# Windowed attention and a rational feed-forward layer on one core: the first 50 transfers of the load queue each wait for an earlier one to land

## The chip, the core and the metric

The kernel runs on one core of a Trainium2 chip. A core has a matrix engine (PE, with its weight loads PEld), two elementwise engines that read PE's accumulators (DVE and ACT), a third that works on on-chip memory only (POOL), and a sequencer (SP) from which this kernel issues all of its data transfers. The metric is the device time of one launch in microseconds, as a median over runs.

## The reference

Eight batches of eight heads of attention, 576 positions of 64 values, each query seeing at most 32 keys (the last 32 positions in the first four heads, every fourth of the last 128 in the other four). The result, 4608 tokens of 512 values, goes through a feed-forward layer with a rational activation.

```python
scores = scale * np.matmul(q, k.transpose(0, 1, 3, 2))
...
scores = np.where(masks[None, :, :, :], scores, -1000000000.0)
...
attn = attn / (np.sum(attn, axis=-1, keepdims=True) + 1e-09)
return np.matmul(attn, v).astype(np.float32)
...
h = x @ w_in
...
P = a[0] + a[1] * h + a[2] * h2 + a[3] * h3
Q = 1.0 + np.abs(b[0]) * np.abs(h) + np.abs(b[1]) * h2
g = P / (Q + 1e-06)
return (g @ w_out).astype(np.float32)
```

The weights w_in (512 x 2048) and w_out (2048 x 512) arrive in 64 bit.

## The kernel before

**Tiling.** Attention is cut into 48 units, six to a batch. A unit loads a tile `qk` (448 KB) and a tile `v`, PE makes the scores into the accumulator tile `pair` (`pair_A` and `pair_B` in the first batch), DVE and ACT make the softmax, PE turns the weights (`t`) and multiplies by `v`, and the result is split into a high and a low part, `xh` and `xl`. The feed-forward layer is cut into 144 tiles: 12 matmuls make `h` (512 tokens by 128 hidden values), ACT, DVE and POOL make the activation, split into `gh` and `gl`, and 12 matmuls add it into four accumulators `out`. All matmuls of that layer run as three products of split values.

**Weights.** 32 slices of the weights (`wi_raw` and `wo_raw`, 512 KB each) are loaded in 64 bit. ACT scales the upper words (`wi_f<-wi_raw`), ACT or POOL scales the lower words (`wi_raw<-wi_raw`), DVE joins them, and two more operations split the result into a high and a low part.

**Order.** Every operation is an `Op` of a planner, class `Plan`. The table `ORDER` lists, by number, in which order operations are placed and, by a letter, on which engine; what it doesn't list is placed by the planner's own rule at the end. `place` calls the function that writes the instructions, so the program of each engine is in that order. The planner's model of time decides two further things: which of several equal buffers a tile gets (`held`), and how many filler matmuls `keep_busy` puts on PE where the model sees PE idle for longer than 0.25 us in the first 150 us (`idle`). Fillers write `ident_b` or zeros into an accumulator and change no result.

**Transfers.** `load` (line 337) issues a transfer on SP, in program order. A transfer waits for what it reads or overwrites; besides, the completion semaphores are eight, used in turn, and a transfer waits before it takes a semaphore of which the transfer eight places ahead has not landed. So up to eight transfers lie in the queue. The planner's model has the same limit, `FLYING = 8`, and a model of how PE's program is fetched in pages of 256 instructions: a page is asked for at one place of the program, comes `FETCH` later, and PE waits for it at another (`PAGE`, `ASK`, `LAST`).

Of the kernel before, what the change touches and what calls it, by code (L numbers as in the profile page):

```python
# [26 lines left out]
BOTH = {"ACT": 375, "DVE": 465}  # L27


START_S, START_O = ["A", "att"] * 3, ["B", "B", "B", "A", "B", "A"]  # L30
KIND = [0, 0, 0, 0, 1, 0] + [2] * 6
LESS = [0, 0, 0, 0, 1, 1]
# [73 lines left out]
1642 507 548 549 1671 550 1672 1656p 543 1639 551 552 1659 1658 508p 1660 1673a 1674d 538 1682 594 1677 1686 553 544 554 558 526 527p 559 565 555 560  # L106
566 567 613 1691 568 569 1657 1692 1693d 561 1678 1687 556 1675 1694 570 1696 1680 1695p 1697 1698 1689 571 1699 572 576 1700 1709 562 1690 1676 1701
573 1702 1681 1710 577 578 595 1711p 1713p 1727 579 1712 545 1714 1715 1703a 1704p 563 1716 574 1683 1717 1707 1728 584 546p 1718 1705 1708 1730 1706
632 1684 1729p 564p 1719 1720 1721a 1745 1732 1731p 580 1733
""".split()  # L110


class Op:
# [4 lines left out]
    def __init__(self, engs, rank, fn, deps, dma, lock):  # L118
        self.engs, self.rank, self.fn, self.dma, self.lock = engs, rank, fn, dma, lock
        self.deps = [d for d in deps if d is not None]  # L120
        self.takes, self.follows = [], []
        self.words, self.parts = 0, 1
        self.spare = None
        self.slack, self.by, self.end, self.eng, self.tail = None, None, None, None, 0.0
# [8 lines left out]
class Plan:  # L133
# [5 lines left out]
    DUE_HOP, WINDOW = 150.0, 200.0  # L139
    PE_START = 1500.0  # L140
    DMA_START, DMA_NS, DMA_RATE, DMA_FIRST = 1000.0, 1100.0, 355.0, 1100.0
    FLYING, PAGE, ASK, LAST, FETCH = 8, 256, 150, 449, 7400.0
    PERIOD, PE_LATE = 4743.0, 105.0

    def __init__(self, idle):
        self.ops, self.tags, self.idle, self.now = [], {}, idle, {}

    def op(self, engs, rank, fn, *deps, dma=0, lock=False, words=0, tail=0.0, parts=1):
        o = Op(engs, rank, fn, deps, dma, lock)
# [49 lines left out]
    def run(self, order):  # L199

        free, pages, flying = {}, [], []
        state = {"pipe": 0.0, "ports": 0.0, "words": 0, "left": len(self.ops)}
        left, after = {}, {}
        for o in self.ops:
            before = o.deps + [f for f in o.follows if f]
            left[id(o)] = len(before)
            for d in before:
                after.setdefault(id(d), []).append(o)
        ready = {id(o): o for o in self.ops if not left[id(o)]}

        def options(o):
            queue = []
            if o.dma:
                parts = 0
                for f in reversed(flying):
                    if parts + f.parts + o.parts > self.FLYING:
                        queue = [f.end]
                        break
                    parts += f.parts
            for eng, ns in o.engs.items():  # L220
                shared = state["ports"] if Plan.shares(o, eng) else 0.0
                held = [t for _, t, _ in self.held(o, eng)]
                start = max([free.get(eng, 0.0), shared] + queue + held + [d.after(eng) for d in o.deps])
                if start < math.inf:
                    yield start, o, eng, ns

        def fetched(start, ns, words):

            n0, n1 = state["words"], state["words"] + words
            for n in range(n0, n1):  # L230
                at = start + ns * (n - n0) / words
                if n % self.PAGE == self.ASK:
                    pages.append(at + self.FETCH)
                if n % self.PAGE == self.LAST - self.PAGE and n >= self.LAST and pages[n // self.PAGE - 1] > at:
                    ns += pages[n // self.PAGE - 1] - at
            state["words"] = n1
            return ns

        def place(start, o, eng, ns):
            self.now = {tag: n for tag, _, n in self.held(o, eng)}  # L240
            for tag, users in o.takes:
                self.tags[tag][self.now[tag]] = users
            o.eng = eng
            if eng == "PE":
                if start > free.get(eng, 0.0) + 1.0:
                    ns += self.PE_LATE
                    since = free.get(eng, self.PE_START)
                    fetched(since, start - since, 2 * self.idle(o, since, start))
                ns = fetched(start, ns, o.words)
            free[eng] = start + ns  # L250
            if Plan.shares(o, eng):
                state["ports"] = start + ns
            o.end = start + ns
            if o.dma:
                flying.append(o)
                state["pipe"] = max(state["pipe"], o.end + self.DMA_START) + o.dma / self.DMA_RATE
                if len(flying) == 3:
                    state["pipe"] += self.DMA_FIRST
                o.end = state["pipe"] + self.DMA_NS
            del ready[id(o)]  # L260
            state["left"] -= 1
            o.fn(eng)
            for n in after.get(id(o), []):
                left[id(n)] -= 1
                if not left[id(n)]:
                    ready[id(n)] = n

        for item in order:
            n, eng = (int(item[:-1]), ENGINES[item[-1]]) if item[-1] in ENGINES else (int(item), None)
            o = self.ops[n]  # L270
            assert id(o) in ready, "the order breaks a dependency"
            place(*next(x for x in options(o) if eng in (None, x[2])))
        while ready:
            every = [x for o in ready.values() for x in options(o)]
            assert every, "the plan is stuck"
            first = min(x[0] for x in every)
            eng0 = min((x for x in every if x[0] == first), key=lambda x: x[1].rank)[2]
            place(*min((x for x in every if x[2] == eng0 and x[0] <= first + self.WINDOW), key=lambda x: (x[1].rank, x[0])))
        assert not state["left"], "the plan is stuck"
# [3 lines left out]
def tile_attention_moe(  # L283
# [10 lines left out]
    nc = tc.nc  # L294
# [8 lines left out]
    pin = tc.keep_in_program_order  # L303
# [30 lines left out]
    plan = Plan(idle)  # L334
    op = plan.op

    def load(dst, src):
        pin(nc.sync.dma_start(dst, src))

    def mm(o, lhs, rhs, start=True, stop=True, free=False):  # L340
        pin(nc.tensor.matmul(o, lhs, rhs, start=start, stop=stop, skip_group_check=free))  # L341
# [44 lines left out]
    class Unit:  # L386
# [6 lines left out]
        def load_qk(self, pool, tag):  # L393
            t = pool.tile([P, RQ + RKEY], F32, tag=plan.at(tag), name=f"qk{self.n}", bufs=1)
            load(t, qk[self.n])
            self.q = t[:, :RQ].rearrange("p (g i c) -> p g i c", g=4, i=3)
            self.k = t[:, RQ:].rearrange("p (g k) -> p g k", g=4)

        def load_v(self, pool, tag):
            if self.n:  # L400
                self.v = pool.tile([P, NBAND if self.start else NV], F32, tag=plan.at(tag), name=f"v{self.n}", bufs=1)
                load(self.v, vb[self.n - 1] if self.start else vp[self.n - NU])
                return
            t = pool.tile([P, NBAND + NMASK + 6], F32, tag=tag, name="v0", bufs=1)
            load(t, head)
            self.v = t[:, :NBAND]
            extra["mask"] = t[:, NBAND : NBAND + NMASK].bitcast(BF16).rearrange("p (m k) -> p m k", k=64)
            extra["coef"] = t[:, NBAND + NMASK :]
# [857 lines left out]
```

## Time and profile before

| | |
|---|---|
| median of 3 runs | 893.29 us (890.53 to 895.08) |
| the profiled execution | 891.1 us, of which the span of its instructions is 889.1 us |
| granted PE clock | 1.00 of full speed |
| busy: PE, PEld, DVE, ACT, POOL | 875.1, 710.0, 722.9, 661.4, 499.7 us |
| moved by transfers | 102.63 MB, mean 115 GB/s over the span |

Busy time is counted from the span's start. A share over the whole span hides that the first 75 us are of another kind than the rest; stages have to be read by windows.

### The profile page before, as it was taken

The numbers are of one execution on the slowest core, as the hardware profiler recorded it, in microseconds if no ns is written. First come the engines' busy times: TensorE is split into PE (matmuls) and PEld (weight loads), VectorE is DVE, ScalarE is ACT, GpSimd is POOL, SyncE is SP. The second block draws the span as 40 slices with busy tenths as digits, with TensorE's granted clock in tenths as the row PEclk, the third lists the DMA queues.
The fourth block names the chain that finished last, engine by engine and source line by source line (L and its number), as shares of the span: only waits on it lengthen the run. The fifth ranks groups of instructions, "written<-read, shape, count | busy, mean of one in ns | idle before, by whom it ended". The sixth has DMA issues, their size and how long they took to land.

```text
span 889.1 us, 20736 instructions
## 1 busy us (share of the span) xinstructions
PE 875.1 (98%) x7991; PEld 710.0 (80%) x7991; DVE 722.9 (81%) x1285; ACT 661.4 (74%) x1104; POOL 499.7 (56%) x462
## 2 busy tenths in 40 slices
PE   7999999999999999999999999999999999999998
PEld 4777888888787888888888888888888887888886
DVE  6999899998898988888897889887666677667656
ACT  4999987776468876777776776777777787777764
POOL 4577767767565655556555464545554445444442
PEclk9999999999999999999999999999999999999999
DMA  9986451338853444443453435221200020001001
GB/s 349 344 260 204 175 203 36 105 109 244 247 157 101 137 139 148 128 134 114 149 162 96 134 107 175 79 80 38 81 11 1 1 71 1 1 1 47 1 1 47
DMA packets 85186, 102.63 MB, mean 115 GB/s; under 512 B 37216, under 2 KB 62560, under 8 KB 85088
## 3 DMA queue, kind: packets, MB, share of 16 engines
q1 hardware_dynamic: 85088, 101.32, 35.4%
q8 instruction: 62, 1.02, 0.5%
q14 instruction: 36, 0.29, 0.1%
HBM read 74.42 MB, written 26.87 MB: 114 GB/s over the span
## 4 chain that ended last, share of the span: by engine, by line
PE 84%; DVE 7%; ACT 4%; DMA 2%; issue 1%; POOL 1%; SPq 0%; DVEq 0%; ACTq 0%; POOLq 0%
PE out L341 40%; PE h L341 39%; PE pair L341 5%; DVE a L350 1%; ACT r L344 1%; DVE h L350 1%; ACT p L344 1%; PE pair_A L341 1%; DMA pT<-turned 1%; DVE xl L347 1%; ACT xh L344 1%; DVE t L347 0%; DMA results<-y 0%; DVE sm L489 0%; DVE wo_f L350 0%
## 5 line engine op out<-in xcount | busy, mean ns | idle before, releaser
L341 PE MATMUL h<-xh,wi 128*128 128x512 f32 x1136 | 376.7, 393 | 1.5 <-DVE a L350 1.3
L341 PE MATMUL out<-gh,wo 128*128 128x512 f32 x1136 | 351.9, 391 | 0.0
L353 POOL TENSOR_TENSOR a<-r,a 128x512 f32<-128x512 f32 x133 | 172.6, 1298 | 253.3 <-ACT r L344 230.1
L341 PEld LDWEIGHTS h<-xh,wi 128*128 128x128 f32 x1136 | 213.2, 188 | 50.4 <-DVE a L350 3.8
L341 PEld LDWEIGHTS out<-gh,wo 128*128 128x128 f32 x1136 | 211.9, 188 | 44.7
L350 DVE SCALAR_TENSOR_TENSOR a<-a,h 128x512 f32<-128x512 f32 x280 | 191.6, 684 | 61.9 <-POOL gl L353 37.8
L341 PE MATMUL h<-xl,wi 128*128 128x512 f32 x568 | 221.3, 390 | 0.0
L341 PE MATMUL out<-gl,wo 128*128 128x512 f32 x568 | 221.1, 389 | 0.0
L353 POOL TENSOR_TENSOR gl<-a,gh 128x512 fp32r<-128x512 f32 x134 | 177.3, 1323 | 41.9 <-ACT gh L344 40.0
L344 ACT ACTIVATE a<-h 128x512 f32<-128x512 f32 x140 | 83.5, 597 | 112.1 <-PE h L341 101.3
L347 DVE TENSOR_TENSOR t<-t,h 128x512 f32<-128x512 f32 x142 | 96.8, 682 | 59.8 <-ACT t L344 59.1
L341 PEld LDWEIGHTS out<-gl,wo 128*128 128x128 f32 x568 | 106.6, 188 | 22.3
L341 PEld LDWEIGHTS h<-xl,wi 128*128 128x128 f32 x568 | 106.6, 188 | 21.3
L344 ACT ACTIVATE r<-a,ln_bias 128x512 f32<-128x512 f32 x141 | 100.7, 714 | 22.0 <-POOL a L353 20.0
L344 ACT ACTIVATE h<-r,exp_bias 128x512 f32<-128x512 f32 x142 | 98.2, 691 | 21.2 <-DVE t L350 15.0
L344 ACT ACTIVATE t<-h,na_t 128x512 f32<-128x512 f32 x142 | 108.6, 764 | 3.6 <-PE h L341 3.5
L350 DVE SCALAR_TENSOR_TENSOR t<-t,na_t,h 128x512 f32<-128x512 f32 x142 | 105.9, 746 | 4.4
L350 DVE SCALAR_TENSOR_TENSOR h<-t,na_t,h 128x512 f32<-128x512 f32 x142 | 106.2, 748 | 0.0
L344 ACT ACTIVATE r<-a,ab_t 128x512 f32<-128x512 f32 x119 | 97.1, 816 | 3.8
L344 ACT ACTIVATE gh<-a 128x512 fp32r<-128x512 f32 x131 | 82.5, 630 | 23.3 <-PE out L341 19.1
L353 POOL TENSOR_TENSOR xl<-z,xh 128x256 fp32r<-128x256 f32 (+5 forms) x58 | 42.5, 748 | 9.9 <-ACT xh L344 8.5
L353 POOL TENSOR_TENSOR p<-p,sm 128x384 f32<-128x384 f32 x36 | 31.0, 861 | 12.1 <-DVE sm L493 9.1
(131 smaller groups left out, 680.5 us busy)
## 6 DMA issues: line engine op xcount, KB each, us to landing
qk<-in_qk_dram SPq DMA_DIRECT2D x48, 448.0 KB, 5.0
v<-in_vp_dram SPq DMA_DIRECT2D x42, 384.0 KB, 3.9
out_dram<-os SPq DMA_DIRECT2D x36, 256.0 KB, 2.1
wi_raw<-in_w_in_dram SPq DMA_DIRECT2D x16, 512.0 KB, 7.5
wo_raw<-in_w_out_dram SPq DMA_DIRECT2D x16, 512.0 KB, 6.3
results<-y SPq DMA_DIRECT2D x42, 192.0 KB, 2.2
z<-results SPq DMA_DIRECT2D x168, 48.0 KB, 1.9
turned<-u SPq DMA_DIRECT2D x36, 192.0 KB, 2.0
```

The lines of the kernel that those rows point to most:

```text
L341: pin(nc.tensor.matmul(o, lhs, rhs, start=start, stop=stop, skip_group_check=free))
L344: pin(nc.scalar.activation(o, i, func, **kw))
L347: pin(nc.vector.tensor_tensor(o, x, y, op))
L350: pin(nc.vector.scalar_tensor_tensor(o, x, s, y, op0, op1))
L353: pin(nc.gpsimd.tensor_tensor(o, x, y, op))
```

## The change

`gate` names, for a transfer that is about to be placed, an earlier transfer: going back over those already sent, the first one behind which at least 800,000 bytes lie (by the sizes that the planner is given). In the first 50 transfers of the planner (a transfer in four parts counts once) the instruction then gets a dependency on the landing of that one. The planner's model follows, its page time `FETCH` goes from 7400 to 5800 ns, and one number, the last, leaves the table.

```diff
+IN_FLIGHT, FLIGHTS = 800000, 50
...
-632 1684 1729p 564p 1719 1720 1721a 1745 1732 1731p 580 1733
+632 1684 1729p 564p 1719 1720 1721a 1745 1732 1731p 580
...
-    FLYING, PAGE, ASK, LAST, FETCH = 8, 256, 150, 449, 7400.0
+    FLYING, PAGE, ASK, LAST, FETCH = 8, 256, 150, 449, 5800.0
...
+        def gate(o):
+
+            if o.dma:
+                ahead, parts = 0, 0
+                for f in reversed(flying):
+                    if (ahead >= IN_FLIGHT and len(flying) < FLIGHTS) or parts + f.parts + o.parts > self.FLYING:
+                        return f
+                    ahead, parts = ahead + f.dma, parts + f.parts
+
         def options(o):
-            queue = []
...
+            queue = [] if gate(o) is None else [gate(o).end]
...
+            self.placing, self.gate = o, gate(o) if len(flying) < FLIGHTS else None
...
     def load(dst, src):
-        pin(nc.sync.dma_start(dst, src))
+        i = nc.sync.dma_start(dst, src)
+        pin(i)
+        if plan.gate:
+            before = plan.sent[plan.gate][-1]
+            tc.add_manual_dep(i.ins, before.ins.name, mybir.DependencyInfo(mybir.DependencyClass.Sync, mybir.DependencyReason.SCHED_ONLY), reason="short queue")
+        plan.sent.setdefault(plan.placing, []).append(i)
```

The order of instructions is the same on SP, DVE, ACT and POOL. On SP the waits differ. The rows below are the first transfers of the program; DMAHW0 to DMAHW7 are the eight completion semaphores in turn, so DMAHW1 in the first eight rows is the semaphore of the second transfer (`v` from `head`). Before:

```order
L338 DMA qk_154<-in_qk_dram 128x896
L338 DMA wi_raw_191<-in_w_in_dram 128x512
L338 DMA qk_228<-in_qk_dram 128x896
L338 DMA wi_raw_289<-in_w_in_dram 128x512
L338 DMA wi_raw_305<-in_w_in_dram 128x512
L338 DMA qk_314<-in_qk_dram 128x896 [waits DMAHW0_49]
L338 DMA v_348<-in_vb_dram 128x512 [waits DMAHW1_49]
```

Now:

```order
L342 DMA qk_154<-in_qk_dram 128x896
L342 DMA wi_raw_191<-in_w_in_dram 128x512 [waits DMAHW1_49]
L342 DMA qk_228<-in_qk_dram 128x896 [waits DMAHW2_49]
L342 DMA wi_raw_289<-in_w_in_dram 128x512 [waits DMAHW3_49]
L342 DMA wi_raw_305<-in_w_in_dram 128x512 [waits DMAHW4_49]
L342 DMA qk_314<-in_qk_dram 128x896 [waits DMAHW5_49,DMAHW0_49]
L342 DMA v_348<-in_vb_dram 128x512 [waits DMAHW6_49]
```

The fifth to tenth transfers each wait for the one three places ahead of them instead of eight places.

On PE six fillers are added and nothing else moves. Four come between the second tile of `h` and the product of attention weights and `v` that follows it. Before:

```order
L341 MATMUL h_894<-xh_302,wi_371 128x512 x2
L341 MATMUL h_894<-xl_303,wi_371 128x512
L341 MATMUL h_894<-xh_302,wi_371 128x512
L341 MATMUL pair<-v_843,pT_864 32x64 [waits DMAHW0_49,DVE_49,Activation_49]
L341 MATMUL pair<-v_843,pT_864 32x64 x23
```

Now (the other two fillers, of `zeros_b`, stand some 50 rows further, ahead of a transpose `t`):

```order
L350 MATMUL h_894<-xh_302,wi_371 128x512
L350 LDWEIGHTS ident_b
L350 MATMUL out_0_0_916<-ident_b 128x512
L350 LDWEIGHTS ident_b
L350 MATMUL out_0_0_916<-ident_b 128x512
L350 LDWEIGHTS ident_b
L350 MATMUL out_0_0_916<-ident_b 128x512
L350 LDWEIGHTS ident_b
L350 MATMUL out_0_0_916<-ident_b 128x512
L350 MATMUL pair<-v_843,pT_864 32x64 [waits DMAHW0_49,DVE_49,Activation_49]
L350 MATMUL pair<-v_843,pT_864 32x64 x23
```

A few tiles also get another of several equal buffers, so that the same instruction waits for another earlier user.

## Rows read from the trace of the kernel before

**Rows 1.** Busy time by stage. Columns: stretch in us, then its length and the busy us (and instructions) of each engine, the granted clock, the busy share of the transfer engines, GB/s.

```profile
0.00:6.50 6.50, 5.04 (x60) 2.08 (x61) 1.02 (x1) 1.28 (x1) 1.88 (x13) 1.00 0.68 219
6.50:22.00 15.50, 11.69 (x328) 8.78 (x329) 13.97 (x34) 9.55 (x29) 7.74 (x9) 1.00 1.03 403
22.00:43.00 21.00, 19.21 (x408) 14.94 (x407) 19.02 (x48) 19.94 (x57) 10.52 (x14) 1.00 1.00 365
43.00:58.00 15.00, 14.16 (x245) 10.54 (x244) 14.86 (x29) 14.26 (x33) 11.47 (x12) 1.00 0.75 266
58.00:74.40 16.40, 15.72 (x251) 12.37 (x249) 16.16 (x30) 15.30 (x32) 11.34 (x11) 1.00 0.78 239
74.40:889.10 814.70, 809.23 (x6708) 661.32 (x6708) 657.83 (x1148) 601.10 (x955) 456.78 (x406) 1.00 0.31 97
```

**Rows 2.** The chain that ended last, in order of time (start us, us, what), where it goes over from DVE to PE.

```profile
73.02 0.68 DVE h L350
...
73.72 0.70 DVE a L350
...
74.46 3.02 PE h L341 x12
77.48 5.44 PE out L341 x24
82.92 5.44 PE h L341 x24
```

**Rows 3.** Who waited for whom: first all waits of DVE from 6.5 to 74.4 us, then waits of PE in the first 130 us that end with a transfer or with nothing the profile shows ("issue"). Columns: us in total, times, longest us.

```profile
DVE mx L449 <- PE pair_A L341: 4.5, 1, 4.5
DVE y L571 <- ACT p L344: 1.3, 2, 0.9
DVE sm L489 <- ACT bands L344: 0.8, 2, 0.6
DVE t L347 <- ACT t L344: 0.3, 1, 0.3
...
PE pair L341 <- issue: 1.1, 2, 0.9
PE pair_B L341 <- issue: 1.1, 2, 0.7
...
PE pair L341 <- DMA qk<-in_qk_dram: 0.2, 1, 0.2
```

**Rows 4.** Transfers as SP issued them (start us, us of the issue, what): the first, one of 5 us and one of 15 us, two around 37 us, and one of 44 us.

```profile
0.74 0.38 SPq L338 DMA_DIRECT2D qk<-in_qk_dram  x1
5.25 0.66 SPq L338 DMA_DIRECT2D qk<-in_qk_dram  x1
14.98 0.33 SPq L338 DMA_DIRECT2D wo_raw<-in_w_out_dram  x1
36.71 0.68 SPq L338 DMA_DIRECT2D wo_raw<-in_w_out_dram  x1
37.49 0.38 SPq L338 DMA_DIRECT2D qk<-in_qk_dram  x1
43.85 0.38 SPq L338 DMA_DIRECT2D qk<-in_qk_dram  x1
```

**Rows 5.** Time from issue to landing, one transfer each, from views of stretches that hold the issue of that one: in this order the `qk` issued at 0.74, 5.25, 37.49 and 43.85 us, and the `wo_raw` issued at 14.98, 36.71 and 71.36 us. Columns: times, KB, us to landing.

```profile
qk<-in_qk_dram SPq DMA_DIRECT2D x1, 448.0 KB, 3.4
qk<-in_qk_dram SPq DMA_DIRECT2D x1, 448.0 KB, 9.7
qk<-in_qk_dram SPq DMA_DIRECT2D x1, 448.0 KB, 5.2
qk<-in_qk_dram SPq DMA_DIRECT2D x1, 448.0 KB, 4.3
wo_raw<-in_w_out_dram SPq DMA_DIRECT2D x1, 512.0 KB, 7.6
wo_raw<-in_w_out_dram SPq DMA_DIRECT2D x1, 512.0 KB, 4.6
wo_raw<-in_w_out_dram SPq DMA_DIRECT2D x1, 512.0 KB, 3.8
```

**Rows 6.** Where loaded tiles are used (start us, us, engine, what): ACT scales the `wo_raw` issued at 14.98, DVE joins it, PE makes scores of the `qk` issued at 5.25 and at 37.49, DVE takes the maximum of the latter.

```profile
23.83 0.78 ACT L344 ACTIVATE wo_raw<-wo_raw,low_bias 128x512 int32<-128x512 uint32 x1
26.08 0.69 DVE L350 SCALAR_TENSOR_TENSOR wo_f<-wo_f,wo_raw 128x512 int32<-128x512 int32 x1
15.27 0.72 PE L341 MATMUL pair_A<-qk 64*32 64x64 f32 x48
45.13 0.72 PE L341 MATMUL pair<-qk 64*32 64x64 f32 x48
48.93 0.55 DVE L449 TENSOR_REDUCE mx<-pair 128x6 f32<-128x384 f32 x1
```

**Rows 7.** PE stands still in the middle of a run of equal matmuls, with nothing the profile shows to wait for; last, what DVE does at the end of the second of these.

```profile
13.82 0.88 PE L341 MATMUL pair_B<-turned_bands,v 128*64 128x96 f32 x15 [0.42 <-issue]
20.07 0.34 PE L341 MATMUL pair<-qk 64*32 64x64 f32 x13 [0.92 <-issue]
19.84 0.55 DVE L347 TENSOR_TENSOR xl<-pair_B,xh 128x384 fp32r<-128x384 f32 x1
20.49 0.56 DVE L449 TENSOR_REDUCE mx<-pair 128x6 f32<-128x384 f32 x1
```

**Rows 8.** Fillers as they ran before (three of them, the first row); then PE around the places of the new ones, what ACT makes of the tile of `h` that starts at 46.20, and of the transpose that starts at 61.02; last, PE's wait at 74.46.

```profile
6.44 0.82 PE L341 MATMUL pair<-ident_b 128*128 128x512 bf16 x3
46.20 0.47 PE L341 MATMUL h<-xh,wi 128*128 128x512 f32 x1 [0.34 <-DVE a L350]
48.78 0.39 PE L341 MATMUL h<-xh,wi 128*128 128x512 f32 x1
50.15 0.58 ACT L344 ACTIVATE a<-h 128x512 f32<-128x512 f32 x1
61.02 0.53 PE L525 MATMUL t<-ident,p 128*128 128x128 f32 x3
61.73 0.47 ACT L344 ACTIVATE pT<-t 128x384 f32<-128x384 f32 x1
74.46 0.50 PE L341 MATMUL h<-xh,wi 128*128 128x512 f32 x1 [0.73 <-DVE a L350]
```

More of the change, by code (lines that the diff above doesn't have):

```diff
@@ L141 @@
     DMA_START, DMA_NS, DMA_RATE, DMA_FIRST = 1000.0, 1100.0, 355.0, 1100.0
-    FLYING, PAGE, ASK, LAST, FETCH = 8, 256, 150, 449, 7400.0
+    FLYING, PAGE, ASK, LAST, FETCH = 8, 256, 150, 449, 5800.0
     PERIOD, PE_LATE = 4743.0, 105.0
     def __init__(self, idle):
-        self.ops, self.tags, self.idle, self.now = [], {}, idle, {}
+        self.ops, self.tags, self.idle, self.now, self.sent = [], {}, idle, {}, {}
     def op(self, engs, rank, fn, *deps, dma=0, lock=False, words=0, tail=0.0, parts=1):
@@ L209, in run @@
         ready = {id(o): o for o in self.ops if not left[id(o)]}
-        def options(o):
-            queue = []
[L213 to L219, printed above, removed]
+        def gate(o):
[5 more added lines that the diff above has]
+                    ahead, parts = ahead + f.dma, parts + f.parts
+        def options(o):
+            queue = [] if gate(o) is None else [gate(o).end]
             for eng, ns in o.engs.items():
```

## The prediction, written before the result was known

> **What bounds the kernel now.** I read the stages first [rows 1]. From 74.4 us to the end PE is busy 809.2 of 814.7 us: nothing that a load does can shorten that part, and its length is the same work after the change. So the time is the moment at which PE's unbroken run begins, plus a constant. That moment is 74.46 us, and the chain that ended last comes to it through DVE [rows 2]: from 6.5 to 74.4 us DVE is busy 64.0 of 67.9 us (13.97 + 19.02 + 14.86 + 16.16) [rows 1]. Then the waits [rows 3]: apart from the 4.5 us before the first scores (which end in the first stretch), DVE waits 2.4 us in all, always for ACT, never for a load. PE waits 0.2 us for a `qk`, and 2.2 us for "issue". Last the transfers: from 6.5 to 22 us they move 403 GB/s with the transfer engines fully busy, from 22 to 43 us 365 GB/s at a share of 1.00, and less after that [rows 1]. A `qk` that is issued into the full queue at 5.25 lands 9.7 us later; the first one, on an empty queue, after 3.4 us [rows 4, 5]. The queue is served at its full rate and most of the 9.7 us is waiting in line.
>
> **The change, part by part.**
>
> *Landing under the gate.* A load that waits in line before SP instead of in the queue lands no sooner, since those ahead of it are the same. It lands no later as long as the queue doesn't run dry. At 403 GB/s a `qk` (458,752 bytes) takes 1.14 us of the queue and a weight slice (524,288 bytes) 1.30 us. A gated load is issued when load f has landed, with typically two loads behind f. If the queue never dries it lands three loads' service after f: 3.4 us (three `qk`) to 3.9 us (three slices), 3.65 us in the middle. If it runs dry, it lands its own lone time after the issue: 3.4 us for the first `qk`, 3.8 us for the `wo_raw` of 71.36 us, and 4.3 us for the `qk` of 43.85 us [rows 5]. So the excess per link is 0 where the rows of the same size are compared (3.4 against 3.4, 3.8 against 3.9), and 4.3 - 3.65 = 0.65 us at worst. I take 0.12 us, near the low end, because two of the three lone times show none. A link spans three transfers, so the first 35 transfers, which SP issued by 37 us, make about 12 links. By then the loads are late by 12 x 0.12 = 1.4 us, with bounds of 0 and 12 x 0.65 = 7.8 us. After 43 us the loads use two thirds of the rate [rows 1], the queue is often short already, and the lag goes away.
>
> *What the lag costs.* The tightest users: the `qk` of 5.25 lands at 14.95 and PE takes it at 15.27, 0.3 us later; the `wo_raw` of 14.98 lands at 22.6 and ACT takes it at 23.83, 1.2 us later; the `qk` of 37.49 lands at 42.7 and PE takes it at 45.13, 2.4 us later, and DVE comes to its scores only at 48.93, another 3 us on [rows 4 to 6]. By those places the central lag is 3 x 0.12, 6 x 0.12 and 1.4 us: 0.4, 0.7 and 1.4 us, which leaves PE 0.1 us late once and ACT not at all. I put 0.2 us for it. The slices are also used by ACT before DVE joins them (23.83 against 26.08), which is a second cover. If the cover is gone, at 7.8 us, the loads around 40 us overrun 2.4 + 3 us by some 2.4 us on DVE's path, and the tight ones around 22 us (half that lag, 3.9 against 1.2 and 2.2 us) cost some 1 to 2 us before: 4 us, and 6 us if ACT, which is busy 19.94 of 21.00 us there [rows 1], passes on what it loses.
>
> What SP queues behind a gated load are later loads and, from 36 us, the small stores and reads by which attention results are turned (`results`, `z`). They lay behind the same loads in the queue before, so they land with the same lag and no other.
>
> *PE's program.* PE stops for 0.42 us at 13.8 and for 0.92 us at 20.07 in the middle of equal matmuls [rows 7]. That fits a page of its program coming late (the planner has a model of such pages). If a short queue lets pages come sooner, PE gains up to 1.3 us. DVE gains little of it: at 20.49 it takes scores that PE finished at 20.41, but its operation before that ended at 20.39 [rows 7], so 0.1 us there and perhaps as much at the other place. I take 0.2 us; bounds 0 and 1.3 us. The Trainium skill speaks against a gain at all: the page "DMA: Bandwidth & Descriptors", section "Queues, rings and completion order", has each transfer engine go round between the queues it has work for, packet by packet, so a page would not stand behind the whole load queue and would come no sooner from a short one. By it this term is 0 and the sum 0.2 us higher; the page "Runtime: NRT & Kernel Launch", section "Instruction fetch mechanics", calls the fetch mostly hidden, and the 0.92 us row says that here it isn't.
>
> *Fillers.* Three took 0.82 us [rows 8], so four take 1.1 us and two 0.55 us. The four delay the `h` that starts at 46.20, where PE idles 0.34 us now, by 0.8 us; it ends at about 49.2, and ACT takes it at 50.15 [rows 8]: hidden. The two come before the transpose of 61.02, which ends at 61.55 and is taken by ACT at 61.73 [rows 8]: up to 0.4 us late, on an engine that is nearly full. I put 0.3 us; if ACT's slack is larger it is 0, and all six on the path would be 1.65 us. PE itself has 0.73 us to spare at 74.46 [rows 8].
>
> *The rest* (the number that leaves the table, page time, other buffers) moves no instruction of DVE, ACT, POOL or SP and costs nothing.
>
> *Sum:* 0.2 - 0.2 + 0.3 = +0.3 us on a span of 889.1, so 889.4, or 891.4 us for an execution like the profiled one (891.1). The median of the runs stands 2.2 us above that one (893.29), so 893.6 us.
>
> **Rivals.**
>
> *The queue starves* (slower). Lone times near 4.3 us rule, each link loses 0.5 to 0.65 us, and the loads come 6 to 8 us late by 40 us. For it: the one lone `qk` in the middle of other work took 4.3 us, not 3.4. Against: `wo_raw` took 3.8 us at 71.36, and 4.6 us at 36.71 although others were still ahead of it [rows 5]. It decides when the lag passes the 2.4 + 3 us of cover at 45 us. Price 4 to 6 us: 899 us. A milder form, 0.3 us a link and 3.6 us late, breaks only the 1.2 us cover of ACT around 23 us and costs 1.5 to 3 us: 896 us.
>
> *Pages come early and DVE's chain follows* (faster). PE's 1.3 us are won and the whole stage slides: 893.29 - 1.3 = 892 us, and with the "issue" waits of [rows 3] gone altogether (2.2 us) 891 us. Against: DVE waits for PE nowhere after the first scores [rows 3].
>
> *The change does nothing.* SP waits for engines, not for the gate, and the queue is as long as before. Against: before, the first eight are issued at once, and 9.7 us latencies show the queue full. It gives 893.3 us, like the forecast.
>
> **How the numbers follow.** Forecast with the variant that nothing happens, 892 to 895.5 us: 0.72. Mild starving: 0.10. Starving: 0.12. Pages and DVE: 0.06. 0.5% is 4.5 us, about what a measurement of this kernel can tell from no change (its three runs span 4.5 us). Slower by that much: the starving case, mostly: 0.11. Faster by it: no term reaches it, and run noise leaves 0.03. The range reaches to the mild case and into the starving one, and down to the early pages with the runs' spread: 890 to 898.5 us.
>
> **What would show it.** Right: SP's loads of the first 22 us land 3.5 to 5 us after the issue instead of 7 to 10; GB/s in 6.5 to 22 us stays above 385; DVE's waits show no load and hardly change; PE's unbroken run begins within 1 us of 74.5. The page step: the stop of 0.92 us is gone or below 0.3. Wrong: GB/s near 350 in that stretch with waits of ACT, POOL or PE for `wi_raw`, `wo_raw` or `qk` of more than 2 us in sum, and the run of PE beginning at 78 or later; or a start before 73, which would mean that a short queue also makes the loads themselves faster.

## The result, and the profile after

The changed kernel is slower: 904.61 us (median, 903.34 to 905.65) against 893.14 us for the kernel before in the same comparison, a ratio of 1.0131 with a 95% interval of 1.0106 to 1.0156. The forecast was no change, 893.6 us, and its range ended at 898.5 us. The profiled execution has a span of 903.1 us, 14.0 us more than the one of before (889.1); the medians differ by 11.5 us, and the single executions of either kernel scatter by 2 to 5 us.

The stages come first, cut as in [rows 1]; the last two rows are stretches inside them (columns as there).

```profile
6.50:22.00 15.50, 11.04 (x324) 8.14 (x319) 13.37 (x32) 8.88 (x27) 7.22 (x8) 1.00 0.89 302
22.00:43.00 21.00, 15.81 (x296) 12.93 (x293) 13.47 (x36) 14.21 (x44) 7.87 (x12) 0.77 0.85 275
43.00:58.00 15.00, 14.14 (x243) 10.42 (x243) 13.89 (x29) 13.46 (x31) 9.20 (x9) 0.98 0.78 248
58.00:74.40 16.40, 12.79 (x184) 9.34 (x183) 11.82 (x24) 12.02 (x31) 7.56 (x8) 1.00 0.78 244
26.60:30.00 3.40, 3.12 (x57) 2.96 (x58) 1.89 (x4) 1.89 (x6) 0.60 (x1) 0.50 0.70 231
36.80:43.60 6.80, 6.23 (x113) 5.34 (x114) 3.23 (x10) 4.12 (x12) 3.14 (x4) 0.50 0.85 253
```

The last column tells it: 302 and 275 GB/s where [rows 1] have 403 and 365, a quarter less in both stretches. DVE, which was busy 19.02 of 21.00 us from 22 to 43 us, is busy 13.47. And TensorE's granted clock is at half, which is 1.2 GHz, in three stretches: the two last rows, and 74.4 to 77.8 us. It was full in every stretch of [rows 1].

Next the chain that ended last, in order of time (start us, us, what). In [rows 2] it came to PE's unbroken run through DVE.

```profile
1.18 3.65 DMA v<-in_head_dram
...
4.84 5.21 DMA wi_raw<-in_w_in_dram
...
10.07 4.80 DMA wi_raw<-in_w_in_dram
...
14.89 5.50 DMA v<-in_vb_dram
...
20.41 6.42 DMA qk<-in_qk_dram
...
26.90 4.23 DMA qk<-in_qk_dram
...
31.14 6.09 DMA v<-in_vp_dram
37.23 0.14 issue
37.37 2.29 PE pair L350 x97
...
57.93 4.67 DMA wo_raw<-in_w_out_dram
...
62.67 5.06 DMA left<-l
...
67.79 2.70 DMA results<-y
...
87.73 3.01 PE h L350 x12
```

Read the start times: from 1.18 to 37.23 us it is one transfer behind another, each issued within 0.1 us of the landing that it waited for, and no engine's work between them. Six links from 4.84 to 37.23 us take 5.4 us each. This is what a closed gate looks like in a chain: the loads wait for themselves. From 57.93 us the same comes back, and its last piece is a `results` store. PE's unbroken run begins at 87.73 us, where [rows 2] have 74.46: 13.3 us of the 14.0. The rest of the program is about as long as it was: 889.1 - 74.46 = 814.6 us before, 903.1 - 87.73 = 815.4 us now.

Then who waited (all engines, 6.5 to 88 us; us in total, times, longest us):

```profile
POOL wi_raw L868 <- DMA wi_raw<-in_w_in_dram: 7.8, 4, 3.3
...
DVE mx L458 <- PE pair_A L350: 4.6, 1, 4.6
DVE mx L458 <- PE pair L350: 4.2, 3, 2.1
...
DVE y L580 <- DMA results<-y: 3.2, 1, 3.2
...
ACT wo_raw L353 <- DMA wo_raw<-in_w_out_dram: 2.3, 1, 2.3
...
PE pair L350 <- DMA qk<-in_qk_dram: 2.1, 4, 0.9
...
PE pair L350 <- DMA v<-in_vp_dram: 1.8, 1, 1.8
```

Before, DVE waited 2.4 us for ACT and never for a load, and PE 0.2 us for a `qk` [rows 3]. Now POOL, ACT and PE all wait for loads, the longest time 3.3 us, and DVE waits for the scores that PE makes late (4.2 us; the 4.6 us ahead of the first scores were there before), and for a store of its own `y`.

Last, from issue to landing, for the transfers issued from 6 to 24 us (times, KB, median us):

```profile
qk<-in_qk_dram SPq DMA_DIRECT2D x4, 448.0 KB, 4.4
wi_raw<-in_w_in_dram SPq DMA_DIRECT2D x3, 512.0 KB, 5.0
```

It fell from the 9.7 us of a full queue [rows 5], but not to the 3.4 us of the lone first `qk`. This is the number that the prediction had put at 3.4 to 3.9 us.

### The profile page after: what moved, and what is told of

It reads as the page before. It is cut to its first block, busy times and chain, and to the rows that moved or that the text cites. A ratio compares the mean times of both kernels' runs of the same rounds, so it can differ in the third digit from the quotient of the medians.

```text
span 903.1 us, 20751 instructions
## 1 busy us (share of the span) xinstructions
PE 882.4 (98%) x7997; PEld 715.2 (79%) x7997; DVE 723.5 (80%) x1285; ACT 662.2 (73%) x1104; POOL 498.8 (55%) x462
## 4 chain that ended last, share of the span: by engine, by line
PE 85%; DMA 7%; DVE 3%; ACT 2%; SPq 1%; issue 1%; POOL 0%; DVEq 0%; ACTq 0%; POOLq 0%
PE h L350 40%; PE out L350 39%; PE pair L350 6%; DMA qk<-in_qk_dram 1%; DMA wi_raw<-in_w_in_dram 1%; SPq L342 1%; DMA results<-y 1%; DVE a L359 1%; DMA z<-results 1%; DMA v<-in_vp_dram 1%; DMA v<-in_vb_dram 1%; ACT r L353 1%; DMA left<-l 1%; DVE h L359 1%; DMA wo_raw<-in_w_out_dram 1%
```

## The experiments

Theory A: the waits starve the queue, since a load issued with two in front takes about 5 us to land, whatever the rate. Theory B: the waits are harmless and something else in the change costs the time (the planner's numbers, the fillers, other buffers). Theory C: it isn't the loads, but SP standing at a wait while small transfers of attention results are queued behind it. Theory D, raised when the half clock was seen: PE loses the time at 1.2 GHz.

In seven of the runs the waits are set apart from the planner's times by a function of their own; the constants change from run to run. The model of the planner stays that of the change, except in `waitonly`:

```diff
+DEP_BYTES, DEP_FROM, DEP_TO, DEP_LEAST = 800000, 0, 50, 0
...
+        def held_back(o):
+            if o.dma and DEP_FROM <= len(flying) < DEP_TO and o.dma >= DEP_LEAST:
+                ahead = 0
+                for f in reversed(flying):
+                    if ahead >= DEP_BYTES:
+                        return f
+                    ahead += f.dma
...
-            self.placing, self.gate = o, gate(o) if len(flying) < FLIGHTS else None
+            self.placing, self.gate = o, held_back(o)
```

**nowait: everything of the change but the waits**

```diff
-        if plan.gate:
+        if False:
```

> The changed kernel with its planner's model, its six fillers and its buffers, but no transfer waits for the gate. Theory A (the queue starves: a load issued behind two others takes about 4.9 us to land, three loads' service is 3.65 us, so every link of the chain loses 1.2 us): the waits are all of the loss, 893 us, within 2 us of before. Rival B (the side effects do it: fillers delay PE, other buffers make other waits): 904 us as the changed kernel.

Measured: 891.89 us against 892.31, ratio 0.9996 (0.9985 to 1.0008). Its stages (columns as above):

```profile
6.50:22.00 15.50, 11.85 (x339) 9.05 (x337) 14.09 (x35) 10.28 (x31) 8.32 (x10) 1.00 1.03 403
22.00:43.00 21.00, 19.14 (x398) 14.91 (x393) 18.68 (x48) 19.77 (x57) 10.53 (x13) 1.00 0.96 356
```

With the waits gone the rates of before are back, and so is the time. Fillers, buffers and the planner's numbers together cost nothing that this run can tell (its interval ends 0.08% above no change): B falls.

**waitonly: nothing of the change but the waits**

The kernel before, with `held_back` above at 800,000 bytes and the wait in `load`; planner numbers, fillers and table stay as they were.

> The kernel before, with its model, fillers and buffers, plus the same waits on SP. Theory A: 904 us, as the changed kernel, with loads 8 us late at the 24th transfer. Rival B: 893 us.

Measured: 905.00 us, ratio 1.0145 (1.0121 to 1.0170), PE's run from 87.15 us on. The waits alone make all of the loss.

**w500, w1200, w1600: how much may lie ahead of a load**

`DEP_BYTES` is 500,000, 1,200,000 or 1,600,000; the rest is as in the diff above.

> The changed kernel with the waits set for 1,200,000 bytes instead of 800,000 (three loads lie behind the awaited one, where there were two; model, fillers and buffers unchanged). Theory A: a link now spans four loads, 4.9 us of service against 4.9 to 5.3 us to land, so the loads are 0 to 3 us late and most of that is covered: 893 to 896 us, GB/s from 6.5 to 22 us back above 380. Rival C (the loss comes from SP standing at a wait while small transfers of attention results are queued behind it, whatever the depth): about half of the loss stays, 898 to 900 us.

> The changed kernel with the waits set for 1,600,000 bytes (four loads lie behind the awaited one). A link spans five loads, 6.1 us of service. Theory A (a load issued into a short queue lands about 5.1 us later, 3.2 us for the first of the 16 transfer engines and 1.6 us more for the last; what of that is not covered by the loads in front is lost at every link): nothing is lost, and one late transfer engine of up to 1 us is covered too: loads at most 1 us late at the 24th, 892 to 895 us. Rival C (SP standing at waits in front of small transfers): 896 us or more.

> The changed kernel with the waits set for 500,000 bytes (one slice, or two other loads, behind the awaited one). Theory A: a link of two to three loads takes about 4.5 us, 1.9 us per load instead of 1.2, so the loads are some 14 us late at the 24th and 22 to 25 us at the 35th: 913 to 922 us. Rival C: SP waits oftener, but for the same small transfers, 905 to 909 us.

Measured:

| bytes ahead | time, us | ratio (95%) | GB/s, 6.5 to 22 us | PE's run from, us |
|---|---|---|---|---|
| 500,000 | 916.43 | 1.0276 (1.0253 to 1.0299) | 252 | 97.18 |
| 800,000 (the change) | 904.61 | 1.0131 (1.0106 to 1.0156) | 302 | 87.73 |
| 1,200,000 | 898.36 | 1.0075 (1.0046 to 1.0104) | 368 | 79.30 |
| 1,600,000 | 893.10 | 1.0004 (0.9987 to 1.0021) | 398 | 74.91 |
| no wait (`nowait`) | 891.89 | 0.9996 (0.9985 to 1.0008) | 403 | 73.98 |

The ratios are what compares, since each run has its own comparison with the kernel before. From 1,600,000 bytes down every smaller queue is slower; `w1600` and `nowait` can't be told apart. At 1,200,000 bytes A's number, 893 to 896 us, was missed, and 898.36 us lies where C had put it (898 to 900 us). `w1600` decides between them: C gave 896 us or more, A 892 to 895, and 893.10 us was measured. So A stands as a mechanism. The chain that ended last in `w1200` shows where its number went wrong (start us, us, what):

```profile
12.29 5.03 DMA qk<-in_qk_dram
17.33 5.04 DMA qk<-in_qk_dram
22.43 7.18 DMA wi_raw<-in_w_in_dram
...
29.68 1.16 POOL wi_raw L877
```

Links of 5.0 us would just do with more bytes in each. In the one of 7.18 us a single transfer engine lagged (in the trace's records the fifteenth of the sixteen was done 5.13 us after the issue), and that cost 2 us that never came back. It is only a part of the miss: against the trace of before, the 17th transfer, ahead of that lag, lands 1.0 us late, the 18th, the first that it held up, 3.4 us, and the 35th 6.0 us. This queue had nothing in reserve for a late landing, and it lost some time without one. That is the reading of one execution; the runs of this kernel reach from 896.46 to 903.47 us.

At 1,600,000 bytes the stages are those of before:

```profile
6.50:22.00 15.50, 11.98 (x340) 8.71 (x325) 13.87 (x34) 9.56 (x29) 7.53 (x9) 1.00 1.02 398
22.00:43.00 21.00, 19.57 (x407) 15.33 (x408) 19.03 (x50) 20.14 (x59) 11.23 (x14) 1.00 1.00 358
```

This run also tells what PE's stops are worth. The stop of 0.92 us [rows 7] is gone: the 48 matmuls run in one piece. The other stop of [rows 7], 0.42 us there, is not gone (timeline of PE).

```profile
14.00 0.88 PE L359 MATMUL pair_B<-turned_bands,v 128*64 128x96 f32 x15 [0.39 <-issue]
18.77 0.72 PE L359 MATMUL pair<-qk 64*32 64x64 f32 x48
```

DVE takes the scores at 20.49 us, as before, since its operation ahead of that one ends no sooner:

```profile
20.49 0.55 DVE L467 TENSOR_REDUCE mx<-pair 128x6 f32<-128x384 f32 x1
```

So a shorter queue takes the longer stop away, and there is no gain that the run can tell (1.0004). In `nowait`, with the full queue, the stop is there (0.76 us). That it is a page of PE's program that comes late fits this, but no row shows it.

In the smallest queue the larger loads took no less to land than in the change's own (issued from 6 to 24 us, `w500`):

```profile
qk<-in_qk_dram SPq DMA_DIRECT2D x4, 448.0 KB, 4.6
wi_raw<-in_w_in_dram SPq DMA_DIRECT2D x3, 512.0 KB, 5.0
v<-in_vb_dram SPq DMA_DIRECT2D x4, 256.0 KB, 3.0
```

4.6 and 5.0 us at 252 GB/s, 4.4 and 5.0 us at 302 GB/s: for loads of 448 and 512 KB the time of a landing didn't fall any more between these two queues, and the rate fell instead. Only the `v` of 256 KB landed sooner, 3.0 us against 4.8 us in the change.

**first22 and after22: the early waits and the late ones**

`first22` gives the first 24 transfers that the planner places their waits (`DEP_TO = 24`), `after22` those from the 25th to the 50th (`DEP_FROM = 24`).

> The changed kernel with the waits in the first 24 transfers only, all of them loads; the later ones, among them all small transfers of attention results, have none. Theory A: the loads are 8 us late at the 24th, and DVE and ACT with them; the later ones catch up in part: 898 to 901 us. Rival C: SP stands in front of no small transfer, 893 to 895 us.

> The changed kernel with the waits only from the 25th transfer of the planner on. Theory A: the first 24 land as before; the later ones, 15 loads and the small transfers between them, lose about 4 us by the 35th where 2 to 4 us are covered, and DVE may still wait for a store of results that stands behind a gated load: 894 to 899 us, less loss than with the first 24 alone. Rival C: all of the loss is here, 902 to 905 us.

Measured: 899.88 us, 1.0088 (1.0053 to 1.0123), and 897.88 us, 1.0059 (1.0044 to 1.0074). Within their intervals the halves add up: 0.88% and 0.59% make 1.47%, the change has 1.31% and `waitonly` 1.45%. C doesn't account for it: in `first22` no small transfer waits, and the loss is there (C gave 893 to 895 us), and `after22` has less than all of it (C gave 902 to 905 us). The late half costs 5 us although the rate there was already below the queue's best; in its waits of DVE stands (us, times, longest)

```profile
DVE y L589 <- DMA results<-y: 2.8, 1, 2.8
```

which `first22` doesn't have at all. So a part of what C names is real in the late half.

**loadsonly: no wait for the small transfers**

`DEP_LEAST = 262144`: the `results` stores and `left` have no wait of their own. The size that counts is the planner's, and `z` stands there with 326,608 bytes, so `z` keeps its wait, other than the expectation says.

> The changed kernel in which only loads of qk, v and weights have the wait; stores and reads of attention results and the small remainders have none of their own, though they still stand behind gated loads in SP's program. Theory A: 901 to 904 us, the same but for the 3 us for which DVE waits for a store of results. Rival C (a small transfer's own wait is what costs): 897 us or less.

Measured: 902.73 us, 1.0113 (1.0098 to 1.0128). DVE's wait for the store is still there:

```profile
DVE y L589 <- DMA results<-y: 2.6, 1, 2.6
```

So the store's own wait isn't what makes DVE wait. What holds the store shows in the changed kernel: first SP's issues, then DVE's instructions (start us, us, what).

```profile
63.14 0.44 SPq L342 DMA_DIRECT2D qk<-in_qk_dram  x1
65.05 0.33 SPq L342 DMA_DIRECT2D wo_raw<-in_w_out_dram  x1
67.79 0.33 SPq L342 DMA_DIRECT2D results<-y  x1
```

```profile
59.85 0.64 DVE L580 STREAM_TRANSPOSE y<-pair 128x192 f32<-128x192 f32 x2
...
70.58 0.65 DVE L580 STREAM_TRANSPOSE y<-pair 128x192 f32<-128x192 f32 x2 [3.19 <-DMA results<-y]
```

`y` is done at 60.49 us and its store is issued at 67.79, 7.3 us later. For the first 4.9 us it stands on SP behind loads that wait for landings, the last of them the `wo_raw` of 65.05; the other 2.4 us are its own wait, for the `left` that lands at 67.72 (chain above). In `loadsonly` the store follows its `wo_raw` at once, but takes 5.12 us to land instead of 2.70:

```profile
64.15 5.12 DMA results<-y
```

What the missing wait saved was spent in the queue, and DVE's wait is only 0.6 us shorter. DVE can't write the next `y` until the store has read the buffer, and in the changed kernel waits 3.19 us. Against the trace of before the first of these transposes is 8.0 us late (51.84 there), the second 12.6 us (58.02 there). What this wait costs by itself no run isolates: it would need another order of the issues.

**keepclk: the clock held up**

```diff
+            if 3 <= self.n <= 11:
+                for _ in range(8):
+                    mm(self.s[:, 0, :192], zeros_b, ident_b[:, :96].unsqueeze(1).to_broadcast([P, 2, 96]), start=False, stop=False, free=True)
```

> The changed kernel with eight more fillers (zeros added to the scores, 192 columns each, about 0.1 us) ahead of the matmuls of the scores in units 3 to 11, so that PE is busy in part of the time in which it would wait for a qk. In the changed kernel the granted clock fell to 1.2 GHz in three stretches, 13.6 us together, in which PE was busy 12.8 us. Theory A (late loads set the path; the clock adds little): the clock stays up in more of the stage, the time does not get better than 902 us, and fillers that come after a qk has landed may cost up to 2 us: 902 to 907 us. Rival D (half the work of those stretches was lost to the clock and is on the path, up to 6 us): 897 to 900 us, if the granted clock stays at 2.4 GHz.

Measured: 904.52 us, 1.0133 (1.0110 to 1.0156). Its stages:

```profile
6.50:22.00 15.50, 12.89 (x356) 10.42 (x349) 13.74 (x33) 9.64 (x29) 7.26 (x8) 1.00 0.92 315
22.00:43.00 21.00, 17.06 (x360) 13.91 (x356) 15.42 (x43) 16.70 (x52) 8.20 (x11) 1.00 0.84 282
43.00:58.00 15.00, 13.99 (x245) 11.01 (x223) 14.12 (x25) 12.53 (x25) 10.89 (x11) 1.00 0.82 275
```

The granted clock is 1.00 where the changed kernel had 0.77 (half remains in one stretch, 71.0 to 74.4 us), the rate is nearly as low as there, and the time is the same, where D gave 897 to 900 us. The half clock came with PE's waiting and isn't what made the kernel slower: D falls. A gain of up to 2 us that the added fillers took back (the price that the expectation gave them) isn't excluded.

## Why the prediction was wrong

**The landing time: the step that failed.** The prediction said that a load with two in front lands 3.4 to 3.9 us after its issue, or at worst 4.3 us, and put the excess per link at 0.12 us, "near the low end, because two of the three lone times show none". In the sum that became +0.2 us; PE's run begins 13.3 us late. The same transfers that land from 10.1 to 37.2 us in the changed kernel, five links, land from 10.1 to 29.1 us in the trace of before: 8.2 us over five links, 1.6 us each, two and a half times the upper bound. The lone times were the wrong comparison: a gated load has two in front that are still moving. The form "three services, or the lone time, whichever is longer" was wrong with it: the medians are 4.4 us (`qk`) and 5.0 us (`wi_raw`), more than either, and the links of the chain take 4.2 to 6.4 us. Nor were all three lone: when the `wo_raw` of 71.36 was issued, the `qk` of 66.69 was still on its way (it landed at 72.0). Rows of the right kind stood in [rows 5]: the `wo_raw` of 36.71, with a slice and a `v` in front that landed at 38.4 and 39.3 us, took 4.6 us, and the `qk` behind it 5.2 us. That is what the gate gave. The prediction named the 4.6 us, as an argument against the rival.

How much must be in flight can be estimated from rate times landing time. With the landing times of `qk` that is 302 GB/s x 4.4 us = 1.3 MB in the change, 252 x 4.6 = 1.2 MB in `w500`, 398 x 6.1 = 2.4 MB in `w1600` (median of four `qk` issued from 6 to 22 us). At the full 403 GB/s and a landing time of 4.4 us, the shortest of these medians, 1.8 MB would be the least. `w1200`, at 368 x 5.4 = 2.0 MB, still lost 9% of the rate, so by this estimate the need lies between 2.0 and 2.4 MB.

**"After 43 us ... the lag goes away."** It grew. The 24th transfer lands 8.1 us later than before (38.5 against 30.4 us), the 35th 12.0 us (53.3 against 41.3), and the store that was issued at 52.50 us before lands 14.5 us later (70.5 against 56.0). Nor did it go away where the waits end: in `first22`, in which nothing behind the 24th transfer waits, PE's run begins at 82.92 us, 8.5 us late. The prediction took the lower use of the rate for a queue with room; but waits that make each load stand for an earlier landing cost there too, 5.2 us in `after22`.

**"They land with the same lag and no other."** This was said of the small stores behind gated loads on SP. In the queue of before they lay behind loads that were being moved; on SP they stand behind loads that haven't been issued. The store that was issued 0.02 us after its `y` before (52.48 and 52.50) was issued 7.3 us after it, and DVE waited 3.2 us for its buffer. The prediction named what is queued behind the gate, but didn't ask who reuses the buffer.

**The cover.** The places it named for a late load (0.3 us at PE, 1.2 at ACT, 2.4 + 3 at 45 us) were right as places; they were weighed one by one against a lag of 1.4 us. Against a lag of 8 us and growing they don't matter: all are gone, and loads are the chain.

**The rival** "the queue starves" named the mechanism, and its signs, given as those of a wrong forecast, came one by one: a rate under 350 GB/s (302), waits for loads over 2 us, PE's run after 78 us. It was priced at 899 us and given 0.12. The price was too low for the reasons above: it had at most 0.65 us a link, it let the lag end at 43 us, and it had no wait for the store.

**What held.** The time is the start of PE's run and nearly a constant: 814.6 us before, 815.4 in the change, 913.6 - 97.18 = 816.4 in `w500`, and at most 817.5 in any of the runs. Fillers, buffers and the planner's numbers cost nothing that can be told (0.9996); the 0.3 us that the prediction put for the fillers is below what the run can resolve. Of PE's stops the one of 0.92 us goes in a shorter queue, the one of 0.42 us stays near what it was in `w1600`, and no gain shows (1.0004; the predicted 0.2 us is below what the run can resolve).

**What stays open.** Why a landing takes near 5 us with two in front and not 3.6. In the records of these transfers (medians of the 6th to the 23rd) the first of the 16 transfer engines is done 3.2 us after the issue and the last 5.1 us; for the very first `qk` of the kernel before it is 2.75 and 3.36 us. So 0.5 us of the excess is a later first engine and 1.3 us a wider spread. In the trace of before the spread is as wide (7.2 and 8.75 us); there the engines that are done presumably go on with the next load, which under the gate hasn't been issued. This was read from records and not tried in a run.

None of the versions is faster than the kernel before; `w1600` and `nowait` can't be told from it.

## What to carry to other kernels

A long landing time in a full queue is no waste by itself: read the rate first. Where the transfer engines were busy all the time, as here, none of the shorter queues gained anything, and those of 1,200,000 bytes and less lost. Before a load is made to wait for a landing, multiply the full rate by the landing time of a load that has others in front (never by that of a lone one), and keep clearly more than that in flight. And list what stands behind the waiting issue on its engine: a small store held there keeps a buffer, and through it an engine that had nothing to do with the loads.

## What the runs showed of the hardware

With 0.8 MB ahead, the `qk` loads of 448 KB took 4.4 us to land and the `wi_raw` loads of 512 KB 5.0 us (medians), and no less with 0.5 MB ahead (4.6 and 5.0 us); the first load of the program, a `qk` on an empty queue, took 3.4 us in the kernel before and 3.2 us in the changed one. The Trainium skill, page "DMA: Bandwidth & Descriptors", section "Latency and other measured facts", gives 0.2 us on average and 2 us at high load for an access to the chip's main memory, and calls it the larger part of a transfer's fixed time. A fixed time that grows under load agrees in direction with 3.4 against 4.4 us, but the 4.4 us also hold the moving of the loads in front, and no run here shows whether the memory has a part in it.

The granted clock of the changed kernel fell from 2.4 to 1.2 GHz for 3.4, 6.8 and 3.4 us, each time behind a stretch in which PE had stood still more than before. The stretch ahead of the first fall (columns as in the stages):

```profile
22.00:26.60 4.60, 2.21 (x35) 1.50 (x31) 3.14 (x11) 2.67 (x9) 2.19 (x4) 1.00 0.88 276
```

PE is busy 2.21 of 4.60 us there; in the trace of before it is 4.02. Ahead of the other two falls it is busy 4.84 us from 30.0 to 36.8 us (before 6.55), and 1.70 us from 70.5 to 74.4 us (before 3.22). The half clock behind these stretches cost nothing that the median shows (1.0133 with the clock held up in all but one stretch, 1.0131 without).
